# Attention with an MLP gate: rows of maxima turned by four operations and moved by two transfers, maxima 20 steps ahead instead of 22

## The chip, the cores and the metric

The kernel runs on one core of one Trainium2 chip. The metric is the device time of one execution in microseconds; shown is the median of three runs.

## The reference

x is 2048 x 512. It is normalized over its rows (layernorm without weights), goes through an attention of 32 heads that share one head of keys and one of values (head size 16), and through an MLP with the Mish activation (512 to 1792 to 512). The output is x plus the attention times the SiLU of the MLP.

```
xn = layernorm(x)
q = (xn @ wq) as 32 heads of 16;  k = xn @ wk;  v = xn @ wv      # k and v: 2048 x 16
s = softmax(q k^T * 16**-0.5) v, heads joined, @ wo
h = xn @ w1 + b1;  g = silu((h * tanh(softplus(h))) @ w2)
out = x + s * g
```

All of it is fp32. The scores are large, so each row of the softmax needs its maximum.

## The kernel before

**Tiling.** The queries are cut into 4 chunks of 512 (C, NC). A unit v is four heads of one chunk, so there are 32 units (NU). Its queries lie in one of three tiles qt: 64 partitions for half a = 0, 64 for a = 1, and two slices p side by side, so (p, a) is one head. The 2048 keys are 16 tiles of 128. One step, s = 16 v + k, is the work of unit v on key tile k; there are 512 steps (NS).

**What a step does.** TensorE makes four score matmuls `e` (L1090), each 128 keys x 512 queries of one head, ScalarE takes their exponentials (L1095) into tiles pts, and four value products `pv` (L1176) add them up two steps later. The scores must come out with the row's maximum already taken off. For that the maximum of each query is needed before its unit begins, so the scores are computed a second time, with the queries on the partitions: matmuls `m` (L1118), four to a step and 64 to a unit, and VectorE's reduce of each (L1122, 128 x 512 to one column of mb). These run LEAD = 22 steps (L34) ahead of the `e`. PSUM has three banks for them.

**Rows of maxima.** When a unit's 64 columns are there, `c_rows` (L1134 to L1163) makes of them two rows for each head (a rounded maximum and its remainder, negated, which the score matmul adds by two more rows of its contraction). `top_rows` (L1567) issues its parts one per step: `reduce` (L1141), `parts` (L1144, L1146), and last `turn` and `move` together. `turn` is one 32 x 32-block transpose on VectorE of a 128 x 32 tile (L1151), `move` eight transfers on the SyncE queue (L1161) that set the rows into partitions 48, 49 and 112, 113 of the unit's qt. The first `e` of the unit waits for them.

**Filling.** Matmuls `x` (half matmuls of 64 partitions, `Mm.half`, L122; whole ones, L118) of the projections, of the MLP and of the output projection (groups, each with a post that empties its bank) are put between `e` and `m`. A planner in the builder decides, from a table of due times and from costs, which group runs when: `q_group` (L751) gives the projection of queries a due time from LEAD, `at(16*v - LEAD - 9 + 2*n)` (L769) its loads. A step takes 4, 6 or 8 halves; a group of 13 to 16 matmuls that is due at a step divisible by 4 can run as a `unit` (L684): two pieces of two steps each with 16 halves, in which the eight `e` and eight `m` alternate.

**Beginning and end.** Before the steps, a lead phase (L1475 to L1560) issues by a planner of its own, with tasks and their estimated times, the layernorm, keys, values, the first queries, the maxima of the first steps and first groups of the MLP. It ends when both halves of `m` are 2 * LEAD on (`min(m_next) >= 2 * LEAD`) and the rows of unit 0 are down by its estimate `cdone` (L1522). At the other end no maxima are left for the last LEAD steps: from TAIL = NS - LEAD on, `tail_pair` (L1590) issues steps in pairs of eight `e`, with `x` halves of two groups between them and eight `pv`.

Of the kernel before, what the change touches and what calls it, by code (L numbers as in the profile page):

```python
# [14 lines left out]
F32 = mybir.dt.float32  # L15
# [5 lines left out]
P = 128  # L21
# [9 lines left out]
NFT = F // P  # L31
NKT = S // P
NU = 8 * NC
LEAD = 22  # L34
NWARM = 24
E0 = 76.0
X_US = 9.0
# [91 lines left out]
def block_kernel(ctx: ExitStack, tc: tile.TileContext, x, wq, wk, wv, wo, w1, b1, w2, out):  # L129
    nc = tc.nc  # L130
    cp = ctx.enter_context(tc.tile_pool(name="const", bufs=1))
    sb = ctx.enter_context(tc.tile_pool(name="work", bufs=2))
# [7 lines left out]
    pe, act, dve, pool, sp = nc.tensor, nc.scalar, nc.vector, nc.gpsimd, nc.sync  # L140
# [18 lines left out]
    def sp_at(us):  # L159

        sp_t[0] = max(sp_t[0], us_of(step[0])) + us
        return step_of(sp_t[0] + 2.6) - 1
# [24 lines left out]
    def f(ap):  # L187
        return ap.bitcast(F32)
# [370 lines left out]
    def prepare():  # L559
        for n in range(min(2 if step[0] < NS - LEAD else 8, len(queue))):  # L560
            if queue[n].pre and queue[n].pre():
# [175 lines left out]
    xt_done = {}  # L737

    def q_group(c, b):
        it = item("wq", ("q", b), wq[:, P * b:P * (b + 1)].rearrange("(t p) n -> p t n", p=P))  # L740

        def post(ps):
            qh = sb.tile([P, C], F32R, tag="qh", name=f"qh{c}_{b}", bufs=1)
            ql = sb.tile([P, C], F32R, tag="ql", name=f"ql{c}_{b}", bufs=1)
            first = (c, b) == (0, 0)
            if first:
                act.activation(qh, ps, AF.Copy)
                lead["q"](lambda: sub(dve, ql, ps, f(qh)))
            else:
                act.activation(f(ql), ps, AF.Copy)  # L750
                gap[0] += 1  # L751
                hi_pool(qh, f(ql))
                sub(pool, ql, f(ql), f(qh))
            for k in range(2):
                v = 8 * c + 2 * b + k

                def dmas(v=v, k=k, parts=((0, 0), (0, 1), (1, 0), (1, 1))):
                    q = qt_of[v] = qts[v % 3]
                    for p, a in parts:
                        o = 64 * a  # L760
                        r = 64 * k + 16 * (2 * p + a)
                        for d, src in ((o, qh), (o + 16, qh), (o + 32, ql)):
                            sp_at(0.63)
                            sp.dma_start(f(q[d:d + 16, p]), f(src[r:r + 16]))
                if first:
                    lead["qdma"](dmas)
                else:
                    for n in range(4):
                        at(16 * v - LEAD - 9 + 2 * n, lambda dmas=dmas, n=n: dmas(parts=(divmod(n, 2),)))  # L769

        return Group(mm12(lambda j, a: it.tile[:, a, P * j:P * (j + 1)],
                          lambda j, b_: xt_of[c][:, b_, j], NDT, (c, b) == (0, 0)), post, [it],
                     [lambda: 32 * (4 * c + b) - LEAD - 18, lambda: xt_done.get(c)])

    t_hist = [-10 ** 6] * 2
    xr_hist = [-10 ** 6] * 3
# [275 lines left out]
    for c in range(NC):  # L1052
        for k in range(3):
            a = take(2)
# [79 lines left out]
    def c_rows(v):  # L1134

        mp = sb.tile([P, 2, 3, 8], F32R, tag="mp", name=f"mp{v}", bufs=2)
        mx = f(mp[:, :, 0])
        w = {}

        def reduce():  # L1140
            dve.reduce_max(out=mx, in_=mb_of[v].rearrange("p b (a z) -> p a z b", a=2), axis=AX.X)  # L1141

        def parts():
            dve.tensor_reduce(out=mp[:, :, 1], in_=mx.rearrange("p a (z o) -> p a z o", o=1), axis=AX.X,  # L1144
                              op=ALU.max, negate=True)
            dve.tensor_reduce(out=f(mp[:, :, 2]), in_=f(mp[:, :, 0:2]).rearrange("p a s z -> p a z s"), axis=AX.X,  # L1146
                              op=ALU.add, negate=True)

        def turn():
            cr = w["cr"] = sb.tile([P, 32], F32, tag="cr", name=f"cr{v}", bufs=2)  # L1150
            dve.transpose(cr, f(mp[:, :, 1:3]).rearrange("p a s z -> p a (s z)"))  # L1151

        def move():
            q, cr = qt_of[v], w["cr"]
            if not lead:
                sp_t[0] = max(sp_t[0], us_of(step[0]) + 4.0)
            for a in range(1, -1, -1):
                r = 64 * a + 48
                for b in range(4):
                    sp_at(0.68)  # L1160
                    sp.dma_start(f(q[r:r + 2]).rearrange("o p (t b n) -> b o (p t) n", b=4, n=32)[b],  # L1161
                                 cr[32 * b + 16 * a:32 * b + 16 * a + 16])
        return reduce, parts, turn, move  # L1163

    def pv(s):
# [114 lines left out]
    now = [0.0]  # L1280
# [15 lines left out]
    def task(eng, us, fn, deps=(), **kw):  # L1296
        t = Task(eng, us, fn, deps, **kw)
        plan[eng].append(t)
        return t
# [61 lines left out]
    for c in range(NC):  # L1361
        z = slice(4 * c, 4 * c + 4)
# [110 lines left out]
    cdone = [None]  # L1473
    kind = [None]
    while True:  # L1475
        opts = []
        for e in ("ACT", "DVE", "POOL", "SP"):
            if e == "POOL":
                T[e] = max(T[e], busy[0] + E0)
            if b := best(e):  # L1480
                early = max(now[0], b[1].start(0))
                opts.append((early if e == "DVE" and b[1].prio < 2 and b[0] < early + 5.0 else b[0], e, b[1]))
        b = best("PE")
        m = m_ready(T["PE"])
        if m is not None and b and b[0] < T["PE"] + 0.2 and T["DVE"] > T["PE"] + 1.0:
            m = None
        if m is not None and (b is None or m <= b[0] + 0.05 or T["DVE"] < T["PE"] + 0.3 and m <= T["PE"] + 0.1):
            opts.append((m, "PE", "M"))
        elif b:
            opts.append((b[0], "PE", b[1]))  # L1490
        e0 = min((o for o in opts if o[1] == "PE"), default=None, key=lambda o: o[0])
        low = min((o[0] for o in opts), default=None)
        if e0 is None or e0[0] > T["PE"] + 0.35:
            opts.append((T["PE"], "PE", "X"))
        if not any(o[1] == "ACT" and o[0] < T["ACT"] + 0.1 for o in opts):
            opts.append((T["ACT"], "ACT", "J"))
        s, e, k = min(opts, key=lambda o: o[0])
        if cdone[0] is not None and s >= cdone[0] - 0.4 and min(m_next) >= 2 * LEAD:
            break
        when(s)  # L1500
        for tag in items:
            load(tag)
        if k == "M":
            d = max(T["DVE"], s + 0.45)
            for a in pick[0]:
                if m_next[a] == len(mseq):
                    mseq.append(pick[1])
                    got[pick[1][0]] += 1
                m_one(a)
                d += 0.6  # L1510
                m_ends.append(d)
            T["DVE"] = d
            T["PE"] = s + (0.25 if kind[0] == "M" else 0.45)
            kind[0] = "M"
            if vdone[0] == 0 and got[0] == 32 and m_next[0] == m_next[1]:
                vdone[0] = 1
                r = c_rows(0)
                r1 = task("DVE", 0.9, lambda: (r[0](), r[1](), r[2]()))

                def move():  # L1520
                    r[3]()
                    cdone[0] = now[0] + 4 * 0.65 + 2.0  # L1522
                task("SP", 5.2, move, [r1])
        elif k == "X":
            fresh = cur["g"] is None
            if cur["g"] is not None or not waiting and (vdone[0] or begun[0] < 1 + (s - 18) / X_US) and begin():
                begun[0] += fresh
                fill(3)
                T["PE"] = s + 0.23 * 3 + (0.2 if kind[0] == "M" else 0)
                kind[0] = "X"  # L1530
            else:
                keep_warm()
                T["PE"] = s + 0.25
                kind[0] = "X"
        elif k == "J":
            tag = next((g for g in ("wq", "ws", "wb") if not any(soon(k, s) for k in plan["POOL"]) and arrived(g) and busy[0] + E0 < s + (4.5 if g == "ws" else 0.5)), None)
            n = ran[0]
            if tag:
                split(tag)
                T["ACT"] = s + 0.6  # L1540
            else:
                gap[0] = 0
                if not plan["POOL"]:
                    act_jobs(1)
                T["ACT"] = s + (0.65 if ran[0] > n else 0.15)
        else:
            plan[e].remove(k)
            if k.fill and cur["g"] is None and not waiting:
                keep_warm()
            k.fn()  # L1550
            T[e] = max(s, T[e]) + k.us + (0.15 if e == "PE" and kind[0] == "M" else 0)
            k.end = T[e]
            if e == "PE":
                kind[0] = "T"
# [196 lines left out]
```

## Time and profile before

| | |
|---|---|
| runs | 1561.91, 1559.70, 1562.19 us; median 1561.91 |
| profiled execution | 1561.58 us, its span 1559.8 us |
| TensorE matmul busy | 1548.8 us, 99% of the span |
| VectorE busy | 1348.1 us, 86%; of it 1266.2 in 2048 reduces of maxima |
| ScalarE busy | 1292.6 us, 83%; of it 1064.8 in 2048 exponentials |
| GpSimd busy | 636.3 us, 41% |
| granted TensorE clock | 0.998 of full |

A matmul's time is counted from its start to its modelled end, and matmuls overlap, so the 99% says that TensorE nearly always has something running. It does not say that the pitch of the matmuls could not be shorter. The pitch is read from the chain of waits: its pieces follow each other without gaps.

### The profile page before, as it was taken

The numbers are of one execution on the slowest core, as the hardware profiler recorded it, in microseconds if no ns is written. First come the engines' busy times: TensorE is split into PE (matmuls) and PEld (weight loads), VectorE is DVE, ScalarE is ACT, GpSimd is POOL, SyncE is SP. The second block draws the span as 40 slices with busy tenths as digits, with TensorE's granted clock in tenths as the row PEclk, the third lists the DMA queues.
The fourth block names the chain that finished last, engine by engine and source line by source line (L and its number), as shares of the span: only waits on it lengthen the run. The fifth ranks groups of instructions, "written<-read, shape, count | busy, mean of one in ns | idle before, by whom it ended". The sixth has DMA issues, their size and how long they took to land.

```text
span 1559.8 us, 31423 instructions
## 1 busy us (share of the span) xinstructions
PE 1548.8 (99%) x11715; PEld 864.1 (55%) x11715; DVE 1348.1 (86%) x2280; ACT 1292.6 (83%) x2509; POOL 636.3 (41%) x668
## 2 busy tenths in 40 slices
PE   9999999999999999999999999999999999999998
PEld 6555655655555565565545556555554555655644
DVE  7998888889989988888998988888889999888854
ACT  6588888789888778977989788897788878878796
POOL 4787349366356203331625422163152323314122
PEclk9999999999999999999999999999999999999999
DMA  6334134133231303212113220321321213131020
GB/s 199 104 133 139 46 111 139 30 113 112 87 111 49 108 16 113 72 24 100 52 58 111 92 92 17 104 69 58 111 59 38 100 58 105 30 99 32 19 71 34
DMA packets 71955, 125.47 MB, mean 80 GB/s; under 512 B 19742, under 2 KB 33356, under 8 KB 71804
## 3 DMA queue, kind: packets, MB, share of 16 engines
q1 hardware_dynamic: 71372, 122.68, 24.9%
q8 instruction: 93, 1.52, 0.4%
q10 hardware_dynamic: 432, 0.79, 0.1%
q14 instruction: 58, 0.48, 0.1%
HBM read 75.57 MB, written 26.21 MB: 65 GB/s over the span
## 4 chain that ended last, share of the span: by engine, by line
PE 98%; DVE 1%; ACT 0%; DMA 0%; issue 0%
PE xps L122 45%; PE pv L1176 32%; PE m L1118 10%; PE e L1090 7%; PE xps L118 1%; DVE mb L1122 1%; PE warm L1344 1%; PE kp L356 0%; PE xp L315 0%; PE wop L122 0%; ACT pts L1095 0%; PE y2ps L122 0%; DMA ks<-ks 0%; PE wop L118 0%; ACT hb L808 0%; ACT xt L324 0%
## 5 line engine op out<-in xcount | busy, mean ns | idle before, releaser
L1122 DVE TENSOR_REDUCE mb<-m 128x1 f32<-128x512 f32 x2048 | 1266.2, 683 | 164.2 <-PE m L1118 129.0
L1095 ACT ACTIVATE pts<-e 128x512 f32<-128x512 f32 x2048 | 1064.8, 607 | 218.3 <-PE e L1090 164.0
L1118 PE MATMUL m<-ks,qt 48*128 48x512 f32 (+1 forms) x2048 | 842.3, 422 | 1.2 <-DMA ks<-ks 1.2
L1090 PE MATMUL e<-qt,ks 64*128 64x512 f32 x2048 | 750.9, 406 | 0.2 <-ACT pts L1095 0.2
L1176 PE MATMUL pv<-pts,vaug 128*32 128x512 f32 x4096 | 529.9, 603 | 0.0
L1118 PEld LDWEIGHTS m<-ks,qt 48*128 48x128 f32 (+1 forms) x2048 | 371.1, 185 | 79.5 <-DVE mb L1122 41.4
L1090 PEld LDWEIGHTS e<-qt,ks 64*128 64x128 f32 x2048 | 375.8, 186 | 29.9 <-ACT pts L1095 16.3
L122 PE MATMUL xps<-wbs,act 64*128 64x512 f32 x1270 | 324.6, 399 | 0.0
L122 PE MATMUL xps<-xt,ws 64*128 64x512 f32 x1128 | 312.3, 409 | 1.7 <-ACT pts L1095 0.9
L122 PEld LDWEIGHTS xps<-xt,ws 64*128 64x128 f32 x1128 | 194.4, 185 | 185.7 <-ACT pts L1095 123.3
L122 PEld LDWEIGHTS xps<-wbs,act 64*128 64x128 f32 x1270 | 227.0, 184 | 99.5 <-ACT pts L1095 26.8
L1176 PEld LDWEIGHTS pv<-pts,vaug 128*32 128x32 f32 x4096 | 88.3, 108 | 152.5 <-issue 144.5
L175 POOL TENSOR_TENSOR hb<-hb,t 128x512 f32<-128x512 f32 x56 | 72.2, 1289 | 163.2 <-ACT t L827 89.4
L185 POOL TENSOR_SCALAR t<-t 128x512 f32<-128x512 f32 x56 | 34.4, 614 | 181.5 <-ACT t L814 181.4
L122 PE MATMUL xps<-xt,wq 64*128 64x512 f32 x336 | 93.0, 409 | 0.0
L122 PEld LDWEIGHTS xps<-xt,wq 64*128 64x128 f32 x336 | 57.9, 185 | 55.4 <-ACT pts L1095 37.7
L175 POOL TENSOR_TENSOR oc<-oc,sc 128x512 f32<-128x512 f32 (+1 forms) x16 | 20.6, 1290 | 152.5 <-DMA qt<-qh 49.8
L122 PE MATMUL xps<-wbs,ot_all 64*128 64x512 f32 x288 | 79.3, 408 | 0.0
L122 PEld LDWEIGHTS xps<-wbs,ot_all 64*128 64x128 f32 x288 | 49.5, 184 | 46.9 <-ACT pts L1095 28.5
L175 POOL TENSOR_TENSOR act<-hb,act 128x512 fp32r<-128x512 f32 x56 | 72.1, 1288 | 4.7
L175 POOL TENSOR_TENSOR hb<-hb,u 128x512 f32<-128x512 f32 x56 | 72.2, 1289 | 4.4
L175 POOL TENSOR_TENSOR u<-u,t 128x512 f32<-128x512 f32 x56 | 71.9, 1284 | 4.7
(164 smaller groups left out, 878.6 us busy)
## 6 DMA issues: line engine op xcount, KB each, us to landing
wbs<-w SPq DMA_DIRECT2D x39, 512.0 KB
ws<-w SPq DMA_DIRECT2D x36, 512.0 KB
qt<-qh SPq DMA_DIRECT2D x256, 32.0 KB
w<-wbs SPq DMA_DIRECT2D x14, 512.0 KB
wq<-wq SPq DMA_DIRECT2D x14, 512.0 KB
wbs<-wo SPq DMA_DIRECT2D x12, 512.0 KB
rawws<-in_dram SPq DMA_DIRECT2D x20, 256.0 KB
w<-ws SPq DMA_DIRECT2D x10, 512.0 KB
```

What stands on the lines that cost most here:

```text
L118: self.pe.matmul(ps, self.lhs(), self.rhs(), start=(self.k == 0), stop=(self.k == self.tot - 1))
L122: i = self.pe.matmul(ps, self.lhs()[o], self.rhs()[o], start=(self.k == 0 and self.halves == 0), stop=(self.k == self.tot - 1 and self.hal ...
L175: eng.tensor_tensor(out=o, in0=a, in1=b, op=op)
L185: pool.tensor_scalar(o, o, lim, 0.0, op0=ALU.min, op1=ALU.max)
L1090: pe.matmul(e, ks[o:o + 64, P * k:P * (k + 1)], q[o:o + 64, p], start=True, stop=True)
L1095: x = act.activation(dst, e, AF.Exp, scale=0.25)
L1118: pe.matmul(m, q[o, p, P * t:P * (t + 1)], ks[o, C * kb:C * (kb + 1)], start=True, stop=True)
L1122: return dve.reduce_max(out=mb_of[v][:, kb, z:z + 1], in_=m, axis=AX.X)
L1176: pe.matmul(o[32 * j:32 * j + 32], vaug[:, k], pt, start=(k == 0), stop=(k == 15))
L1344: pe.matmul(warm, qts[0][:, 0, 0:P], qts[0][:, 0], start=True, stop=True)
```

## The change

The maxima run 20 steps ahead instead of 22, and the due times of the query projections are moved so that the sum with LEAD stays 40. `turn` takes the four groups of 32 partitions apart: each 32 x 32 block is transposed by an operation of its own, and all four land side by side in partitions 0 to 31 of cr, which is now 32 x 128. So a row of 128 values lies in one partition, and `move` needs one transfer for each half a instead of four. The lead phase's planner gets other costs for the first of these.

```diff
-LEAD = 22
+LEAD = 20
@@ q_group
-                     [lambda: 32 * (4 * c + b) - LEAD - 18, lambda: xt_done.get(c)])
+                     [lambda: 32 * (4 * c + b) - LEAD - 20, lambda: xt_done.get(c)])
@@ c_rows
         def turn():
-            cr = w["cr"] = sb.tile([P, 32], F32, tag="cr", name=f"cr{v}", bufs=2)
-            dve.transpose(cr, f(mp[:, :, 1:3]).rearrange("p a s z -> p a (s z)"))
+            cr = w["cr"] = sb.tile([32, P], F32, tag="cr", name=f"cr{v}", bufs=2)
+            for b in range(4):
+                z = slice(32 * b, 32 * b + 32)
+                dve.transpose(cr[:, z], f(mp[z, :, 1:3]).rearrange("p a s z -> p a (s z)"))
@@ move
             for a in range(1, -1, -1):
                 r = 64 * a + 48
-                for b in range(4):
-                    sp_at(0.68)
-                    sp.dma_start(f(q[r:r + 2]).rearrange("o p (t b n) -> b o (p t) n", b=4, n=32)[b],
-                                 cr[32 * b + 16 * a:32 * b + 16 * a + 16])
+                sp_at(0.68)
+                sp.dma_start(f(q[r:r + 2]).rearrange("o p (t n) -> o (p t) n", n=P), cr[16 * a:16 * a + 16])
@@ lead phase
-                r1 = task("DVE", 0.9, lambda: (r[0](), r[1](), r[2]()))
+                r1 = task("DVE", 1.2, lambda: (r[0](), r[1](), r[2]()))
...
-                    cdone[0] = now[0] + 4 * 0.65 + 2.0
-                task("SP", 5.2, move, [r1])
+                    cdone[0] = now[0] + 2 * 0.65 + 2.0
+                task("SP", 1.3, move, [r1])
```

The instructions keep their number except for the transposes (32 before, 128 now), the transfers of rows (256 before, 64 now) and two matmuls that keep TensorE warm. Counted between the groups of value products, the steps ahead of the tail are these, with the number of `x` halves in each:

| | before | now |
|---|---|---|
| steps of 6 halves | 333 | 333 |
| pieces of a unit (2 steps, 16 halves) | 62 | 64 |
| steps of 4 halves | 26 | 28 |
| steps of 8 halves | 4 | 0 |
| pairs in the tail | 11 | 10 |

VectorE, at the turn of unit 3 (mp the rows, mb the columns of maxima, cr the turned rows); before:

```order
L1146 TENSOR_REDUCE mp_2753<-mp_2753 128x2x8
L1122 TENSOR_REDUCE mb_2758<-m_0_1_2799 128x1
L1122 TENSOR_REDUCE mb_2758<-m_0_2_2807 128x1
L1122 TENSOR_REDUCE mb_2758<-m_0_3_2815 128x1
L1122 TENSOR_REDUCE mb_2758<-m_1_3_2824 128x1
L1151 STREAM_TRANSPOSE cr_2834<-mp_2753 128x32
L1122 TENSOR_REDUCE mb_2758<-m_1_4_2851 128x1
```

and now:

```order
L1146 TENSOR_REDUCE mp_2799<-mp_2799 128x2x8
L1122 TENSOR_REDUCE mb_2808<-m_0_1_2858 128x1
L1122 TENSOR_REDUCE mb_2808<-m_0_2_2866 128x1
L1122 TENSOR_REDUCE mb_2808<-m_0_3_2874 128x1
L1122 TENSOR_REDUCE mb_2808<-m_1_3_2881 128x1
L1153 STREAM_TRANSPOSE cr_2891<-mp_2799 32x32 x4
L1122 TENSOR_REDUCE mb_2808<-m_1_4_2901 128x1
```

Four transposes stand in a row where one stood, between the last reduce of one step and the first reduce of the next. Of the 32 turns, 22 stand so at the border of two single steps (18 ahead of a step of 6 halves, 4 ahead of one of 4), 8 ahead of a unit's piece (3 of them directly behind `parts`), one in the lead and one in the tail.

TensorE, at the end of the lead phase (xtw and ws are weights of the MLP, `x` with L118 are whole matmuls, L122 begins the steps); before:

```order
L118 MATMUL xps<-xt_175,ws_833 128x512 x3
L1118 MATMUL m_0_8_955<-ks,qt_78 128x512
L1118 MATMUL m_1_8_958<-ks,qt_78 128x512
L1118 MATMUL m_0_9_963<-ks,qt_78 128x512
L1118 MATMUL m_1_9_966<-ks,qt_78 128x512
L118 MATMUL xps<-xt_175,ws_833 128x512 x6
L1118 MATMUL m_0_10_982<-ks,qt_78 128x512
L1118 MATMUL m_1_10_985<-ks,qt_78 128x512
L1118 MATMUL m_0_11_988<-ks,qt_78 128x512
L1118 MATMUL m_1_11_991<-ks,qt_78 128x512
L118 MATMUL xps<-xt_175,ws_833 128x512 x3
L122 MATMUL xps<-xt_175,ws_920 128x512
```

and now:

```order
L1118 MATMUL m_0_7_932<-ks,qt_78 128x512
L1118 MATMUL m_1_7_935<-ks,qt_78 128x512
L118 MATMUL xps<-xt_175,xtw 128x512 x6
L118 MATMUL xps<-xt_175,ws_833 128x512 x12
L1431 MATMUL warm<-qt_79 128x512 x2
L122 MATMUL xps<-xt_175,ws_923 128x512
```

The eight `m` are gone from the end of the lead, the twelve `x` of ws run together, and the steps begin behind two warming matmuls.

ScalarE, at the same place (hb, t: the MLP's activation; wbs: a split weight); before:

```order
L488 ACTIVATE wbs<-rawwb_774 128x512
L823 ACTIVATE t_1_801<-u_1_802,two 128x512
L827 ACTIVATE t_1_801<-t_1_801 128x512
L823 ACTIVATE t_2_894<-u_2_895,two 128x512
L827 ACTIVATE t_2_894<-t_2_894 128x512
L808 ACTIVATE hb_4_1002<-xps,b1c 128x512
L1095 ACTIVATE pts<-e_0_0_1_1010 128x512
```

and now:

```order
L488 ACTIVATE wbs<-rawwb_774 128x512
L823 ACTIVATE t_1_801<-u_1_802,two 128x512
L808 ACTIVATE hb_4_966<-xps,b1c 128x512
L1095 ACTIVATE pts<-e_0_0_1_979 128x512
L1095 ACTIVATE pts<-e_0_1_1_987 128x512
L1095 ACTIVATE pts<-e_1_0_1_995 128x512
L1095 ACTIVATE pts<-e_1_1_1_1001 128x512
L827 ACTIVATE t_1_801<-t_1_801 128x512
L1095 ACTIVATE pts<-e_0_0_0_1018 128x512
L1095 ACTIVATE pts<-e_0_1_0_1026 128x512
L1095 ACTIVATE pts<-e_1_0_0_1034 128x512
L1095 ACTIVATE pts<-e_1_1_0_1040 128x512
```

Three activations of the MLP that ran before L808 now stand among the first exponentials: L827 behind the first four, and L823 with L827 of t_2 behind the next four.

## Rows read from the trace of the kernel before

**Rows 1.** The page: busy time by engine, and the chain's share by engine.
```profile
PE 1548.8 (99%) x11715; PEld 864.1 (55%) x11715; DVE 1348.1 (86%) x2280; ACT 1292.6 (83%) x2509; POOL 636.3 (41%) x668
...
PE 98%; DVE 1%; ACT 0%; DMA 0%; issue 0%
```

**Rows 2.** Waits over the span: engine, line, awaited; us in total, times, longest us.
```profile
PEld m L1118 <- DVE mb L1122: 41.4, 90, 1.6
```

**Rows 3.** Chain of waits from 376 us: start us, us, what; three single steps.
```profile
377.40 1.00 PE pv L1176 x8
...
380.10 0.99 PE pv L1176 x8
...
383.09 1.00 PE pv L1176 x8
...
385.94 0.99 PE pv L1176 x8
```

**Rows 4.** Chain of waits from 541 us, a step of 8 halves.
```profile
542.93 0.99 PE pv L1176 x8
...
546.00 0.99 PE pv L1176 x8
```

**Rows 5.** Chain of waits from 1469 us, a piece of a unit.
```profile
1470.71 1.85 PE pv L1176 x16
...
1476.66 1.85 PE pv L1176 x16
```

**Rows 6.** Timeline of VectorE at the turn of unit 3, 207.9 us: columns as above, [idle before <-releaser].
```profile
207.38 0.68 DVE L1122 TENSOR_REDUCE mb<-m 128x1 f32<-128x512 f32 x1
207.98 0.20 DVE L1151 STREAM_TRANSPOSE cr<-mp 128x32 f32<-128x32 f32 x1
208.44 0.69 DVE L1122 TENSOR_REDUCE mb<-m 128x1 f32<-128x512 f32 x1 [0.25 <-PE m L1118]
```

**Rows 7.** Chain of waits from 56 us: two VectorE operations on different partitions, then a transfer.
```profile
56.49 0.03 issue
56.52 0.42 DVE ks L175
...
59.18 2.52 DMA ks<-ks
```

**Rows 8.** Timeline of VectorE at 380 us: an added operation between two steps' reduces.
```profile
380.06 0.68 DVE L882 TENSOR_TENSOR y<-xps,y 128x512 f32<-128x512 f32 x1
```

**Rows 9.** Chain of waits from 72 us, the end of the lead phase.
```profile
74.31 0.97 PE xps L118 x3
...
75.95 1.59 PE xps L118 x6
...
79.14 0.69 ACT hb L808
79.88 0.50 PE xps L122
```

**Rows 10.** Timeline of ScalarE around the first exponentials.
```profile
75.96 0.71 ACT L823 ACTIVATE t<-u,two 128x512 f32<-128x512 f32 x1
76.70 0.63 ACT L827 ACTIVATE t<-t 128x512 f32<-128x512 f32 x1
...
83.32 2.06 ACT L1095 ACTIVATE pts<-e 128x512 f32<-128x512 f32 x4 [0.37 <-PE e L1090]
```

**Rows 11.** Chain of waits from 1494 us, the end of the tail.
```profile
1540.06 1.85 PE pv L1176 x16
...
1544.50 3.57 PE pv L1176 x32
```

**Rows 12.** Timelines of VectorE, SyncE's queue and TensorE: unit 7's turn, transfers, first score.
```profile
395.50 0.20 DVE L1151 STREAM_TRANSPOSE cr<-mp 128x32 f32<-128x32 f32 x1
...
395.73 5.29 SPq L1161 DMA_DIRECT2D qt<-cr  x8
...
403.87 0.40 PE L1090 MATMUL e<-qt,ks 64*128 64x512 f32 x1
```

## The prediction

> **What bounds the kernel now.** I began with the page. TensorE is busy 99% of the span, and the chain that ended last is 98% TensorE [rows 1]. So what counts is the pitch of TensorE's instructions, step by step, and what VectorE (86% busy) and ScalarE (83%) do matters only where TensorE is held for them. The waits show one such place that the change touches: the `m` matmuls waited for VectorE's reduces 90 times, 41.4 us in all [rows 2]. That is little of 1560 us, but it says that `m` has little room against VectorE.
>
> Then I read the chain for the length of a step, as the distance between two groups of value products. From 377.40 to 380.10 it is 2.70 us for a step of 4 halves; the step from 383.09 to 385.94, with 6 halves, takes 2.85; the one before it, also with 6, from 380.10 to 383.09, takes 2.99 [rows 3]. A step of 8 halves takes 546.00 - 542.93 = 3.07 [rows 4], a piece of a unit (two steps, 16 halves) 1476.66 - 1470.71 = 5.95 [rows 5]. A pair in the tail takes 1544.50 - 1540.06 = 4.44, and behind the last come value products alone, 3.57 [rows 11].
>
> **The change, part by part.** All sums are made against the profiled execution, 1561.58 us with a span of 1559.8. The median of the runs is 1561.91, 0.33 off, so nothing is corrected for it.
>
> *Steps.* Two steps go from the tail to the main part. By the table of steps the main part gets 2 pieces of a unit and 2 steps of 4 halves more and loses 4 of 8 halves: 2 x 5.95 + 2 x 2.70 - 4 x 3.07 = 11.90 + 5.40 - 12.28 = +5.0. The steps of 6 are as many. The tail loses one pair. In the order its pairs that are fuller on one side (9 halves there) are two before and two now, one of them now at the very end. So what goes is a plain pair: -4.4. Steps and tail together: +0.6. Fewer maxima ahead give nothing by themselves, since the work is the same and a step with `m` was already as dense as its halves allow.
>
> *Turns.* Before, the single transpose starts at 207.98, 0.08 before the reduce ahead of it ends (207.38 + 0.68), and takes 0.20; then VectorE idles 0.25 until the first `m` of the next step is ready, and its reduce starts at 208.44 [rows 6]. That idle time is all the cover there is. The four new transposes have the same 32 columns on fewer partitions, so I give each 0.20. How they follow each other no row shows for transposes. If they overlap as this one does with the reduce ahead of it, the pitch is 0.20 - 0.08 = 0.12: the last ends at 207.98 + 0.36 + 0.20 = 208.54, and the reduce, again 0.08 earlier, comes at 208.46, 0.02 late. If each starts only 0.03 after the one ahead has ended, as the two ks operations do, which lie on different partitions [rows 7], the pitch is 0.23: the last ends at 207.98 + 0.69 + 0.20 = 208.87, and the reduce comes at 208.79, 0.35 late. The transposes read four different groups of partitions, so the ks row is the nearer one, and I take 0.35.
>
> What does a reduce that is late by 0.35 cost TensorE? The fourth `m` of a step needs the bank of its first, so it waits for that reduce. A row with a like delay is the y addition, 0.68 on VectorE [rows 8], between the reduces of a step of 4 halves and the next: the step that follows takes 2.99 in place of 2.85, 0.14 longer [rows 3]. With it VectorE has 4 x 0.60 + 0.60 = 3.00 to do in a step of 2.70 (0.60 = 0.68 - 0.08 is the pitch of two operations that overlap), so its reduces fall behind by at most 0.30, of which TensorE passes on 0.14. A turn's 0.35 is at least 0.05 more, and what comes on top is passed on whole: 0.19 or somewhat over. I take 0.22. The bounds are 0 (the 0.12 pitch) and 0.35 (all of it passes through). The turns at the border of single steps are 22: 22 x 0.22 = 4.9. Of the 8 ahead of a unit's piece, five come where VectorE has the slack of eight reduces (8 x 0.60 = 4.8) in 5.95; I cost them at nothing. Three stand directly behind `parts`: 0.1 each. The turn in the tail meets no maxima and costs nothing, as VectorE has few reduces there. Together 4.9 + 0.3 = +5.2, with bounds 0 and 22 x 0.35 + 3 x 0.35 = 8.7.
>
> The Trainium skill, page "VectorE: DVE Perf Modes", section "Two Vector instructions with no wait between them", says that an instruction is held until all earlier ones of the engine are done if its input or its output starts in another group of 32 partitions than that of the last instruction which read or wrote that memory. By that rule the second, third and fourth transpose are held, since their inputs begin in other groups, though their outputs do not; the term stays +5.2 by it, and would be about 0 without it. The ks row agrees, but there input and output change together; no row here shows a change of the input alone.
>
> *Transfers.* Eight become two, so SyncE's queue is free 6 x 0.66 = 4.0 us sooner at each turn (5.29 for eight [rows 12]). Nobody waited for it: it adds and takes nothing, unless the rows come too late, which is a rival below. Moving the due times of the query projections with LEAD keeps their sum and is in the counts of steps.
>
> *Lead phase.* Before, the `x` of ws run in three pieces with `m` between them, then ScalarE's L808 takes 0.69, and the steps begin at 79.88 [rows 9]. Now the twelve follow each other. Three take 0.97 and six 1.59 [rows 9], so a further one takes (1.59 - 0.97) / 3 = 0.21, and nine after the first three end at 74.31 + 0.97 + 1.86 = 77.1. With L808's 0.69 and 0.03 and 0.05 around it (79.14 + 0.69 against 79.88) the steps begin at 77.9: -2.0. The two warming matmuls lie beside L808. The eight `m` that left are done inside the steps and are counted there, since each step makes four either way. But L827 (0.63), and L823 with L827 (0.71 + 0.63), now stand between the first exponentials, where ScalarE had 0.37 idle ahead of four of them [rows 10]. From 0 up to 1.97 - 0.37 = 1.6 comes back; if each group of four has such a gap, 0.63 - 0.37 + 1.34 - 0.37 = 1.2. The scores have banks to run ahead into, so I take 1.1. Lead: -0.9, between -2.0 and -0.4.
>
> The sum: 1561.58 - 0.9 + 5.0 - 4.4 + 5.2 = 1566.5 us. By the bounds of turns and lead it runs from 1560.2 to 1570.5; with a turn at 0.15 to 0.33 and the lead at -0.9 it is 1564.9 to 1568.8, the forecast's own range.
>
> **Rivals.**
>
> A, *the turns are hidden* (not slower). The place is the 0.25 of idle time behind the transpose; the four cost nothing if they start at a pitch of 0.12, and the point from which that decides is a pitch of about 0.15, where the last ends in time for the next reduce to be under 0.1 late. For it speaks the overlap of 0.08 in rows 6; against it the ks row. Then 1561.58 - 0.9 + 0.6 + 0.2 = 1561.5: no change.
>
> B, *the rows come too late.* By the order the first score of most units is two steps nearer to the turn, 5.7 us. For units 7, 10 and 18 that is hard: unit 7's `e` came 403.87 - 395.50 = 8.4 after the transpose started [rows 12], so now 2.7. Four transposes at 0.23, two transfers at 0.66 and a landing: with about 1 us after the issue that just does; with 2.52 as the ks transfer took [rows 7] it does not, and each of the three units is up to 0.8 us late beyond what the first `m` of the step cover. That adds up to 2.4: 1568.9. Against it speaks that three units of 32 are few, and that a transfer to two partitions is small.
>
> C, *the lead's gain stays whole and the turns are free*: 1561.58 - 2.0 + 0.6 = 1560.2. It is faster by more than 0.2% only with a run as low as the lowest shown, 2 us below the profiled one.
>
> **How the numbers follow.** The forecast has 0.55, A 0.30, B 0.08, C 0.07. A measurement of this kernel can tell a change from none from about 0.2% on, 3.1 us; so "same" is 1558.8 to 1565.0. Faster: most of C, 0.06. Same: A, the rest of C and the lowest part of the forecast, 0.33. Slower: the rest of the forecast and B, 0.61. The range has to take in A as well as the forecast and B: 1560.6 to 1569.
>
> **What would show it.** In the profile after, the four transposes of a turn should start 0.23 apart (A: 0.12), the reduce behind them 0.3 to 0.4 later than before, and a step of 6 halves behind a turn should take some 3.05 to 3.1 in place of 2.85. The steps should begin near 77.9, units keep 5.95 and tail pairs 4.44. No wait of `e` for a transfer should appear, or B holds. The forecast is wrong if the steps behind turns keep 2.85, or if a main part without the steps of 8 is longer or shorter than the +5.0 by the counts.

## The result and the profile after

The changed kernel takes 1567.96 us in the median of 6 runs (1566.29 to 1568.74), the kernel before 1560.93 in the median of its 6 (1559.70 to 1563.39). The ratio is 1.0042, 95% interval 1.0031 to 1.0054, so it is slower by some 6.6 us. One execution of a variant below, e7's at 2063.03 us with a granted TensorE clock of 0.654, counts as slow and is left out of its median. The profiled execution of after took 1566.29, its span 1564.4, against 1561.58 and 1559.8: 4.7 us apart. Runs of either kernel lie up to 4 us apart, so the traces are first compared piece by piece.

The page of after has the same engines busy to the same shares, except for VectorE, with 96 transposes more:

```profile
PE 1551.8 (99%) x11717; PEld 862.2 (55%) x11717; DVE 1366.1 (87%) x2376; ACT 1294.3 (83%) x2509; POOL 637.7 (41%) x668
...
PE 94%; DVE 3%; ACT 1%; DMA 1%; issue 0%; SPq 0%; POOL 0%; DVEq 0%; ACTq 0%
```

The chain now runs through VectorE for 3% of the span, where it was 1% [rows 1]. The wait that grew is the one of rows 2:

```profile
PEld m L1118 <- DVE mb L1122: 51.7, 116, 1.4
```

It has 26 more waits and 10 us more. They lie at the turns: within a step behind one there are 24 such waits with 10.6 us, where before there was one with 0.8. This is VectorE's timeline at the turn of unit 3 in after, the same place as [rows 6]:

```profile
212.16 0.68 DVE L1122 TENSOR_REDUCE mb<-m 128x1 f32<-128x512 f32 x1
212.76 0.83 DVE L1153 STREAM_TRANSPOSE cr<-mp 32x32 f32<-32x32 f32 x4
213.53 0.64 DVE L1122 TENSOR_REDUCE mb<-m 128x1 f32<-128x512 f32 x1
```

Four transposes take 0.83 together. Each lasts 0.20, and they start at 212.76, 212.96, 213.18 and 213.39, so 0.21 apart, one behind the other; over all turns the mean pitch is 0.210. The next reduce comes 0.77 after the first of them, where it came 0.46 after the single one: 0.31 late, and its idle time of 0.25 is gone. The chain of waits shows what TensorE makes of it:

```profile
211.73 0.99 PE pv L1176 x8
...
214.71 0.99 PE pv L1176 x8
...
217.56 0.99 PE pv L1176 x8
```

The step of 6 halves with the turn takes 214.71 - 211.73 = 2.98, the next 2.85 again. Where a turn stands ahead of a step of 4 halves, the chain itself goes through the transposes; this is unit 7:

```profile
400.25 0.68 DVE mb L1122
400.93 0.10 DVE cr L1153
...
401.05 0.20 DVE cr L1153
...
401.26 0.20 DVE cr L1153
...
401.47 0.20 DVE cr L1153
401.68 0.58 DVE mb L1122
...
402.30 0.50 PE m L1118
```

One reads it from below: the `m` at 402.30 had to wait for the bank that the reduce at 401.68 emptied, and that reduce for four transposes, each begun 0.01 after the one ahead had ended.

Cut where the groups of value products end, the two profiled executions differ like this (times from the start of the span; a kind's usual length is its median, 2.85 for a step of 6 halves, 2.70 for 4, 3.07 for 8, and 5.97 for a piece of a unit):

| piece | before | after | difference |
|---|---|---|---|
| lead phase, up to the end of the first group of value products | 87.93 | 86.46 | -1.5 |
| steps and pieces, by their numbers and usual lengths | | | +5.1 |
| what steps with a turn take above that | 0.1 | 4.4 | +4.3 |
| what other steps take above that | 4.7 | 6.0 | +1.3 |
| tail, up to the last value products | 52.6 | 47.9 | -4.7 |

The sum is +4.5 of the 4.7. Of the 4.4, the 18 turns ahead of a step of 6 halves have 2.5 (0.14 each), the 4 ahead of one of 4 halves 1.3 (0.33 each), the 8 of units 0.6. The 1.3 of the other steps contain four steps of 6 halves that follow a y addition behind a turn: they take 0.26 more than usual in place of the 0.14 of [rows 3]. That VectorE has not caught up there is the likely reason; no run tries it.

The tail kept its plain pairs of 4.44, as [rows 11]:

```profile
1507.36 1.85 PE pv L1176 x16
1511.79 1.85 PE pv L1176 x16
...
1544.07 1.85 PE pv L1176 x16
1549.12 3.57 PE pv L1176 x32
```

The value products of its last two pairs, of the kind that is fuller on one side, start at 1544.07 and 1549.12, 5.05 apart.

The lead phase of this execution ends at the time that was worked out:

```profile
73.21 3.08 PE xps L118 x12
...
76.31 0.70 ACT hb L808
...
77.05 0.74 PE warm L1431 x2
...
77.84 0.49 PE xps L122
...
80.70 0.52 ACT t L827
...
83.17 0.61 ACT t L823
...
85.47 0.99 PE pv L1176 x8
```

and before, behind the steps' begin at 79.88 [rows 9]:

```profile
86.86 1.06 PE pv L1176 x8
```

The twelve `x` run together and the steps begin at 77.84 in place of 79.88. L827 and L823, which in [rows 10] ran ahead of the first exponentials, now lie in the chain between them, and of the 2.0 won, 1.5 are left at the end of the first value products. One thing differs: the two warming matmuls did not lie beside L808 but waited for it and took 0.74 after it.

The two executions also differ in something that is not the change's. These are the busy times of the engines from 24 to 36 us of the span; the third number from the end is the granted TensorE clock. First before, then after:

```profile
24.00:36.00 12.00, 11.99 (x58) 6.93 (x56) 9.77 (x18) 11.33 (x34) 4.66 (x8) 0.86 0.42 137
24.00:36.00 12.00, 11.54 (x60) 6.35 (x60) 10.69 (x18) 11.85 (x37) 4.59 (x7) 1.00 0.45 145
```

Before stood at the lower level of the clock, 0.50 or 1.2 GHz, for some 3.4 of these us, and after never did. So part of the 2.0 and of the 1.5 is clock; the runs below tell how much.

### The profile page after: what moved, and what is told of

It reads as the page before. It is cut to its first block, busy times and chain, and to the rows that moved or that the text cites. A ratio compares the mean times of both kernels' runs of the same rounds, so it can differ in the third digit from the quotient of the medians.

```text
span 1564.4 us, 31121 instructions
## 1 busy us (share of the span) xinstructions
PE 1551.8 (99%) x11717; PEld 862.2 (55%) x11717; DVE 1366.1 (87%) x2376; ACT 1294.3 (83%) x2509; POOL 637.7 (41%) x668
## 4 chain that ended last, share of the span: by engine, by line
PE 94%; DVE 3%; ACT 1%; DMA 1%; issue 0%; SPq 0%; POOL 0%; DVEq 0%; ACTq 0%
PE xps L122 45%; PE pv L1176 32%; PE m L1118 10%; PE e L1090 6%; DVE mb L1122 2%; PE xps L118 1%; PE wop L122 0%; DVE st L246 0%; DMA pts<-in_dram 0%; ACT pts L1095 0%; ACT pts L217 0%; DVE cr L1153 0%; ACT xf L333 0%; PE wop L118 0%; DVE xt L175 0%
## 5 line engine op out<-in xcount | busy, mean ns | idle before, releaser
L122 PE MATMUL xps<-wbs,act 64*128 64x512 f32 x1270 | 324.1, 399 | 0.0
L122 PE MATMUL xps<-xt,ws 64*128 64x512 f32 x1128 | 312.3, 409 | 1.0 <-ACT pts L1095 1.0
L122 PEld LDWEIGHTS xps<-xt,ws 64*128 64x128 f32 x1128 | 194.3, 185 | 184.5 <-ACT pts L1095 123.2
L122 PEld LDWEIGHTS xps<-wbs,act 64*128 64x128 f32 x1270 | 227.3, 184 | 97.4 <-ACT pts L1095 25.2
L122 PE MATMUL xps<-xt,wq 64*128 64x512 f32 x336 | 92.9, 409 | 0.0
L122 PEld LDWEIGHTS xps<-xt,wq 64*128 64x128 f32 x336 | 57.9, 185 | 55.1 <-ACT pts L1095 37.7
L122 PE MATMUL xps<-wbs,ot_all 64*128 64x512 f32 x288 | 79.4, 408 | 0.0
L122 PEld LDWEIGHTS xps<-wbs,ot_all 64*128 64x128 f32 x288 | 49.5, 184 | 47.0 <-ACT pts L1095 28.5
```

The costliest lines, as they stand in the source:

```text
L122: i = self.pe.matmul(ps, self.lhs()[o], self.rhs()[o], start=(self.k == 0 and self.halves == 0), stop=(self.k == self.tot - 1 and self.hal ...
```

## The experiments

In each, the median is of its own runs, and the ratio is to runs of the kernel before on the same chip, not to the 1560.93 of the first row. Executions of one kernel differ by some 3 us with the granted clock of the whole execution: before, beside e1, took 1559.5 to 1560.2 at 0.999 to 1.000 and 1562.2 to 1563.6 at 0.996 and 0.997. So the table also gives how far the mean of a kernel's runs at 0.999 to 1.000 lies above that of before's runs at the same clock on its chip (for after's own comparison the clocks of before are not known, and e6 has no such run). The last columns are of the profiled execution: its clock from 24 to 36 us, the end of the first group of value products (here called the lead), and the span behind that (without lead).

| kernel | median | ratio, interval | above before, like clock | clock, 24 to 36 us | lead | without lead |
|---|---|---|---|---|---|---|
| before | 1560.93 | | | 0.86 | 87.93 | 1471.9 |
| after | 1567.96 | 1.0042 (1.0031 to 1.0054) | | 1.00 | 86.46 | 1478.0 |
| e1 turns only | 1566.69 | 1.0034 (1.0021 to 1.0047) | 6.2 | 0.57 | 90.50 | 1476.9 |
| e2 three extra, same partitions | 1562.50 | 0.9997 (0.9988 to 1.0006) | 0.0 | 0.57 | 90.32 | 1471.4 |
| e3 three extra, other partitions | 1566.71 | 1.0035 (1.0022 to 1.0048) | 6.6 | 1.00 | 87.26 | 1477.7 |
| e4 six transposes | 1577.62 | 1.0101 (1.0087 to 1.0115) | 17.6 | 0.86 | 87.62 | 1489.2 |
| e5 divided, LEAD 22 | 1562.10 | 1.0011 (1.0002 to 1.0020) | 1.9 | 0.57 | 90.43 | 1472.5 |
| e6 divided, LEAD 20 | 1571.53 | 1.0067 (1.0054 to 1.0081) | | 0.57 | 89.75 | 1482.0 |
| e7 LEAD 20, one transpose, eight transfers | 1564.78 | 1.0029 (1.0017 to 1.0042) | 4.3 | 0.72 | 88.62 | 1476.3 |
| e8 as e6, tail's turn whole | 1563.67 | 1.0022 (1.0012 to 1.0032) | 3.2 | 1.00 | 86.61 | 1475.1 |

In the last column 0.5 can't be told from nothing: before and e2, whose steps take the same, are that far apart. e1 to e3 and e5 have LEAD 22, the others 20.

**e1, the turns alone.** The changed kernel with LEAD put back:

```diff
-LEAD = 20
+LEAD = 22
-                     [lambda: 32 * (4 * c + b) - LEAD - 20, lambda: xt_done.get(c)])
+                     [lambda: 32 * (4 * c + b) - LEAD - 18, lambda: xt_done.get(c)])
```

> The kernel before with the new turn and move alone, LEAD 22: steps of every kind and tail pairs are as many as before. Theory T (the turns cost, because four transposes start 0.21 us apart and make the next reduce 0.32 late): every one of the 22 turns at the border of single steps costs 0.14, three of a unit 0.13, so +3.5 us, ratio 1.0022, and the 22 steps show it in the trace. Rival L (what is slower comes from LEAD 20, that is from the steps): within 0.5 us of before, ratio 1.000.

It measured 1.0034, and 5.0 us more than before without the lead phase. The sign and the theory hold, the size was put too low: the 22 turns cost 0.17 on average (3.7 together), those of units 1.0, and other steps another 0.3. So the turns alone carry five of the six us, and at like clock, with 6.2, nearly all. What LEAD 20 adds to them outside the lead phase is the difference to the changed kernel, 1478.0 - 1476.9 = 1.1.

**e2 and e3, what holds a transpose.** The kernel before with its one transpose, and behind it three more into a tile that nobody reads. In e2 all read partitions 0 to 31, in e3 one reads 32 to 63, one 64 to 95, one 96 to 127:

```diff
             dve.transpose(cr, f(mp[:, :, 1:3]).rearrange("p a s z -> p a (s z)"))
+            sc = sb.tile([32, 96], F32, tag="cs", name=f"cs{v}", bufs=2)
+            for b in range(1, 4):
+                dve.transpose(sc[:, 32 * b - 32:32 * b], f(mp[0:32, :, 1:3]).rearrange(...))             # e2
+                dve.transpose(sc[:, 32 * b - 32:32 * b], f(mp[32 * b:32 * b + 32, :, 1:3]).rearrange(...))  # e3
```

> The kernel before with its one transpose and eight transfers, and three further 32 x 32 transposes behind it, all reading partitions 0 to 31 into a tile that nobody uses. Theory T in its form H (a transpose is held because its input lies on other partitions than the one ahead): here nothing is held, the pitch is 0.12, the next reduce at most 0.05 late, ratio 1.000. Rival N (four transposes cost what four instructions cost, wherever they read): pitch 0.21, next reduce 0.32 late, +3.5 us, ratio 1.0022.

> The same three extra transposes, but reading partitions 32 to 63, 64 to 95, 96 to 127; their outputs on partitions 0 to 31 as in the run beside it. H: held, pitch 0.21, next reduce 0.32 late, 22 x 0.14 + 3 x 0.13 = +3.5 us, ratio 1.0022. N: the same +3.5, no difference to the run with all inputs on one group of partitions. Rival L: ratio 1.000.

VectorE's timeline at the turn of unit 3, first of e2:

```profile
210.30 0.20 DVE L1151 STREAM_TRANSPOSE cr<-mp 128x32 f32<-128x32 f32 x1
210.43 0.34 DVE L1154 STREAM_TRANSPOSE cs<-mp 32x32 f32<-32x32 f32 x3
210.75 1.29 DVE L1122 TENSOR_REDUCE mb<-m 128x1 f32<-128x512 f32 x2
```

and of e3:

```profile
207.66 0.20 DVE L1151 STREAM_TRANSPOSE cr<-mp 128x32 f32<-128x32 f32 x1
207.89 0.63 DVE L1154 STREAM_TRANSPOSE cs<-mp 32x32 f32<-32x32 f32 x3
208.46 0.64 DVE L1122 TENSOR_REDUCE mb<-m 128x1 f32<-128x512 f32 x1
```

The same four instructions take 0.45 to the next reduce in e2 and 0.80 in e3. Over all turns the pitch is 0.104 in e2 and 0.219 in e3. In e2 the next reduce comes no later than before, its step takes no more than 2.85, and the kernel takes the same time (0.9997); in e3 it is 1.0035, as with the change's own turns in e1; the 1.0022 expected was again too low. So not the number of transposes costs, but that each reads another group of 32 partitions than the one ahead. The outputs begin on partition 0 in both. Nor is it that each reads other data than the one ahead, as the extra ones of e2 do not: the reduces read other data each time, from the same partitions, and start 0.60 apart with a length of 0.68. That the group of partitions decides is what the Trainium skill says in "VectorE: DVE Perf Modes", section "Two Vector instructions with no wait between them": a changed start of the input alone is enough to hold an instruction until the earlier ones are done. The prediction had no row for that; these two runs are such rows.

**e4, six transposes.** The changed kernel with its first two transposes done twice:

```diff
-            for b in range(4):
+            for b in (0, 1, 0, 1, 2, 3):
```

> The changed kernel with six transposes in a turn in place of four (the first two done twice). The next reduce comes 2 x 0.21 = 0.42 later still. If, as the prediction had it, what comes on top is passed on whole: 22 x 0.42 = +9.2 us over the changed kernel, 1577 us, steps of 6 halves behind a turn at 3.41. If TensorE takes a share of it, as 0.14 of 0.32 so far: 22 x 0.18 = +4.0 us, 1572 us, such steps at 3.18.

Without the lead phase it is 11.2 above the changed kernel, and the first alternative holds: 9.2 was expected if what comes on top passes whole, 4.0 if TensorE takes a share. The turn of unit 3 in e4:

```profile
214.76 1.29 DVE L1153 STREAM_TRANSPOSE cr<-mp 32x32 f32<-32x32 f32 x6
215.99 0.64 DVE L1122 TENSOR_REDUCE mb<-m 128x1 f32<-128x512 f32 x1
```

The reduce comes 1.23 after the first transpose instead of 0.77, 0.46 later, and a step of 6 halves behind a turn takes 0.60 more than usual instead of 0.14: the whole 0.46. In a step of 6 halves the first 0.3 of lateness cost half or less, everything above it its full length.

**e5, the transposes divided over two steps.** The turns of the change at LEAD 22, two transposes in one step and two with the transfers in the next (`r[2]`, the turn, now takes the blocks to do; that part and LEAD are left out here):

```diff
-            rowq.extend([r[0], r[1], lambda r=r: (r[2](), r[3]())])
+            rowq.extend([r[0], r[1], lambda r=r: r[2]((0, 1)), lambda r=r: (r[2]((2, 3)), r[3]())])
```

> Turn and move as in the change, LEAD 22, but the four transposes done two in one step and two in the next, so that the transfers leave a step later. Theory T: two at a pitch of 0.21 make the next reduce only 0.11 late, which the idle time of VectorE takes but for some 0.02; twice 22 x 0.02 = +0.9 us at most, ratio 1.000 to 1.0006. If the four transposes cost by their number and not by what they delay in one step, +5 us as in the run with the turns alone (ratio 1.0034).

1.0011, a little over the 1.0006 expected at most, and without the lead phase 0.6 above before. The half turns cost 0.3 us together in the trace, where the whole ones of e1 cost 4.7. So the price of a turn is nearly gone once its parts fit under the idle time. At like clock the runs are still 1.9 above before; where that lies the trace doesn't show. Nothing is won on the kernel before.

**e6, the same at LEAD 20.** The rule divides a turn if the unit begins at least three steps later (the line that sets v is left out):

```diff
+            def t1(r=r, v=v):
+                near = 16 * v - step[0] < 3
+                if not near:
+                    r[2]((0, 1))
+                    rowq.appendleft(lambda: (r[2]((2, 3)), r[3]()))
+                else:
+                    r[2]()
+                    r[3]()
+            rowq.extend([r[0], r[1], t1])
```

> The changed kernel (LEAD 20) with the same division of the transposes, except at 12 turns, where a unit's first score is too near or where the turn stands ahead of a unit's piece; there the four stay together. Steps of every kind are as many as in the changed kernel. Theory T: the 20 turns that are divided cost nothing, units 7, 10 and 18 keep 0.14 to 0.4 each, so with +5.0 for steps, -4.7 for the tail and about -1 for the lead it is the kernel before again: 1561 us, ratio 0.9990 to 1.0010. Rival L (LEAD 20 costs): it stays near the changed kernel, ratio 1.003 to 1.004.

This was a miss: 1.0067, worse than the change itself, which neither theory had. The chain in the tail shows why:

```profile
1510.35 1.94 POOL e L893
...
1512.30 3.36 DVE e L901
...
1516.46 0.20 DVE cr L1155
...
1516.91 0.67 SPq L1164
...
1517.63 1.92 DMA qt<-cr
```

The second half of unit 31's turn came one call of `tail_pair` later, and there VectorE's queue had a reciprocal (L901) ahead of it that itself waited for GpSimd. The transfers left at 1516.91, and the first score of unit 31 waited for them. TensorE's timeline, and a window's busy times, where the third number from the end is again the granted clock:

```profile
1512.23 1.92 PE L1178 MATMUL pv<-pts,vaug 128*32 128x512 f32 x16
1519.68 0.89 PE L1090 MATMUL e<-qt,ks 64*128 64x512 f32 x2 [5.53 <-DMA qt<-cr]
...
1523.46 1.92 PE L1178 MATMUL pv<-pts,vaug 128*32 128x512 f32 x16
1520.00:1523.00 3.00, 3.00 (x16) 3.00 (x17) 0.00 (x0) 2.17 (x4) 0.00 (x0) 0.52 0.00 0
```

So this pair takes 1523.46 - 1512.23 = 11.23 in place of 4.44. TensorE stood idle for 5.53 of the 6.8 lost. Behind the idle time its clock was at the lower level (0.50, 1.2 GHz) for some 3 us, and the rest, 1.3, lies in this stretch, where the matmuls of the pair follow each other more slowly.

**e8, e6 with that turn whole.**

```diff
-                near = 16 * v - step[0] < 3
+                near = 16 * v - step[0] < 3 or v == NU - 1
```

> The run with the divided turns at LEAD 20 again, with the turn of unit 31, which stands in the tail, kept together. Theory: of that run's +10.4 us over the kernel before, 5.6 came from that turn alone, whose second half stood behind a chain of ScalarE, GpSimd and VectorE work of the tail, so that a pair took 10.04 in place of 4.44; here the pair is back near 4.45. What is left is LEAD's own +1.2 and the undivided or delayed turns (steps behind turns +1.5, steps behind those +0.7): the time outside the lead phase 1480.2 against 1475.7 of before, 1566 us, ratio 1.0030. If LEAD 20 itself costs nothing and the divided turns cost nothing, as expected of the run before: 1561 to 1562 us. If the tail's loss was not that turn: 1571.

The pair is back at 4.44, and without the lead phase e8 is 6.8 below e6: the whole 11.23 - 4.44, where the expectation, which read the pair as 10.04, had 5.6. The measured 1.0022 has the expected 1.0030 within its interval. Without the lead phase it is 3.2 above before: steps with a turn 1.6, other steps 1.3, and 0.4 by the counts of steps and pairs.

**e7, LEAD 20 with the turn of before.** One transpose and eight transfers at the steps of the changed kernel:

```diff
-            cr = w["cr"] = sb.tile([32, P], F32, tag="cr", name=f"cr{v}", bufs=2)
-            for b in range(4):
-                z = slice(32 * b, 32 * b + 32)
-                dve.transpose(cr[:, z], f(mp[z, :, 1:3]).rearrange("p a s z -> p a (s z)"))
+            cr = w["cr"] = sb.tile([P, 32], F32, tag="cr", name=f"cr{v}", bufs=2)
+            dve.transpose(cr, f(mp[:, :, 1:3]).rearrange("p a s z -> p a (s z)"))
...
                 sp_at(0.68)
-                sp.dma_start(f(q[r:r + 2]).rearrange("o p (t n) -> o (p t) n", n=P), cr[16 * a:16 * a + 16])
+                for b in range(4):
+                    sp.dma_start(f(q[r:r + 2]).rearrange("o p (t b n) -> b o (p t) n", b=4, n=32)[b],
+                                 cr[32 * b + 16 * a:32 * b + 16 * a + 16])
```

> The changed kernel with the one transpose and the eight transfers of before, at the same steps (the planner's costs as in the change). The turns cost nothing: -5.5 us against the changed kernel. But the last of eight transfers lands 5.9 us after the turn begins, and the first score of units 7, 10 and 18 stands 3.0 us behind it: each waits some 2.5 to 3 us, the other units up to 0.2. That is +8 to +11, so 1569 to 1573 us. If rows that land late are hidden (rival), 1561.

Also a miss in size: 1564.78, not 1569 to 1573. The turns cost nothing any more (steps with a turn 0.4 above usual, all of it in units), and units 7, 10 and 18 do wait, but 1.0 to 1.2 each. The chain at unit 7:

```profile
402.60 0.67 SPq L1161
...
403.31 0.65 SPq L1161
...
404.00 0.61 SPq L1161
...
404.66 1.66 DMA qt<-cr
...
406.45 0.47 PE e L1090
```

and the waits over the span have lines that neither before nor after has:

```profile
PE e L1090 <- DMA qt<-cr: 2.1, 3, 0.9
PEld e L1090 <- DMA qt<-cr: 1.0, 1, 1.0
```

The first score waits for four of the eight transfers, not for all: `move` sends the rows of half a = 1 first, and the even step with which a unit begins uses that half alone. Without these 3.2 us e7 would be 1.2 above before outside the lead phase: LEAD 20's own price, as e1 gave it from the other side (1.1).

## Why the prediction was right

*The bound.* The reading that TensorE's pitch by kind of step sets the time, and that VectorE counts where `m` waits for it, gave the main terms. What the sum left out or mis-sized is small and named term by term here.

*Steps and tail.* +5.0 and -4.4 were worked out, +5.1 and -4.7 came. In the two runs that measure LEAD apart from the turns it is about +1.1, of which these counts give 0.4; the rest is in other steps that took longer than usual, which was not forecast.

*Turns.* +5.2 was forecast, with the ks pair as the row for the pitch: 0.23, a reduce 0.35 late, 0.22 a turn. The pitch is 0.21, the reduce 0.31 late, and the turn 0.14 ahead of a step of 6 halves. That is, to 0.01, what the prediction's own rule gives for 0.31: 0.14 for the first 0.30, and what is above it whole, which e4 bore out. A step of 6 halves behind a turn so took 2.98 to 3.00, a little less than the 3.05 to 3.1 named as a sign. Not forecast were the 0.33 ahead of a step of 4 halves, where VectorE is denser, and the loss in the steps behind. In the trace 4.3 lie in the steps with a turn; the turns as a whole cost 5.0 without the lead phase by e1, and 6.2 by its runs at like clock. So the mechanism was right and the sum near, but partly because one price too high and others left out make up for each other.

*Rival A* fell with e2 and e3: hidden transposes exist (e2), but only where all read the same partitions. *Rival B* fell for the changed kernel. These are its two transfers at unit 7:

```profile
401.70 1.36 SPq L1162 DMA_DIRECT2D qt<-cr  x2
```

The unit's first score runs at 404.07 and does not wait for them, and nowhere in the kernel does a score wait for such a transfer. e7 shows that B would have come true with eight transfers. The new turn and LEAD 20 need each other in this sense: the two transfers are what lets the rows arrive in time at LEAD 20.

*Lead.* In the two profiled executions it is -1.5, against -0.9 worked out, and the steps begin at 77.84, against 77.9. That agreement is luck. The table shows that the lead goes with the clock from 24 to 36 us: with LEAD 22 it ends at 87.26, 87.93 and 90.32 to 90.50 where that clock is 1.00, 0.86 and 0.57, and with LEAD 20 at 86.46 to 86.61, 87.62 and 89.75. So at a like clock LEAD 20 gains 0.6 to 0.8, 0.3 and 0.6 to 0.8, which is less than the 0.9. What the steps of this term are worth is read from e4, which has the changed lead phase at the 0.86 of before:

```profile
78.21 0.74 PE warm L1431 x2
...
79.00 0.49 PE xps L122
...
86.63 0.99 PE pv L1176 x8
```

The steps begin at 79.00, so 0.9 earlier than before and not 2.0: the twelve `x` take 3.08 and not 2.83, and the two warming matmuls, which were put at nothing, stand behind L808 with 0.74. From there to the end of the first value products it is 8.62, against 8.05 before (79.88 to 87.93): the activations among the exponentials give back 0.6 and not 1.1. The two errors nearly cancel.

*The total.* Predicted 1566.5, measured 1567.96 in the median, or +4.9 against some +6.6. Without the lead phase the terms gave 5.0 + 5.2 - 4.4 = +5.8, and the two executions are 6.1 apart. Part of what is off is the lead's -0.9, of which 0.3 to 0.8 came: at a like clock the two executions would be 5.3 to 5.8 apart. The rest, about 1 us between that and +6.6, stays open. The clock of the whole execution moves a time by some 3 us, and for the runs of before that this ratio rests on it is not known.

None of the variants beats the kernel before. e2 equals it, and e5 stands 0.1% above it.

## What to carry to other kernels

Small operations on a busy engine are priced by the wait that follows them: look for the idle time behind the place where they stand, and divide them over several such places if they don't fit under one. The transposes here that read different groups of partitions ran one behind the other, so one wide operation isn't the same as its four quarters. And before a piece of work is put off by a step, look at what its engine's queue holds ahead of it there, in the tail above all. Last, where executions of one kernel differ, look at the granted clock stretch by stretch before a difference is put down to a change.

## What the runs showed of the hardware that was not expected

A 32 x 32 transpose takes 0.20 us, as long as a 128 x 32 one, when the one ahead read other partitions; three that read the same partitions are shown with a pitch of 0.10 and 0.16 each. And lead phases with the same LEAD differ by up to 3 us from one execution to the next, although the clock of the whole execution stays at 0.996 to 1.000: TensorE stands at the lower level (0.50, 1.2 GHz) somewhere from 24 to 36 us for none or up to some 10 us of them, by the granted clock of 1.00, 0.86, 0.72 or 0.57 there. What TensorE did ahead of it doesn't tell the executions apart: from 16 to 24 us it was busy for 7.95 of 8 us in before, whose clock fell, and for 7.94 in after, whose clock did not. Why it falls in one and not in the other stays open.
